# Score and value matmuls of a fused attention kernel, grouped by token tile instead of by head, with one fixed order for them on TensorE

## The chip, the cores and the metric

The kernel runs on one core of a Trainium2 chip. The metric is device time in microseconds (us), the median of the timed runs. Five engines work side by side, each through a queue of its own in order: TensorE (PE in the profile, with PEld for its weight loads), VectorE (DVE), ScalarE (ACT), GpSimd (POOL) and SyncE (SP), which issues every DMA here. They wait for each other by semaphores.

## The reference, cut to what matters

```python
B, H, S, D = q.shape                       # 2, 8, 768, 64
k_sum = k.reshape(B, H, nb, 32, D).max(axis=3)     # nb = 24 blocks
v_sum = v.reshape(B, H, nb, 32, D).mean(axis=3)
scores_l = scale * q @ k^T, masked to |i - j| < 16
scores_s = scale * q @ k_sum^T + log(32)
a = softmax over [scores_l, scores_s]
x = a @ [v, v_sum]                          # attention, (B, S, 512)
...
xk, xr = mixes of x with its left neighbour (mu_k, mu_r)
x = sigmoid(xr @ w_r) * (relu(xk @ w_k) ** 2 @ w_v)
...
u = x + (relu(x^T @ w_tok1) @ w_tok2)^T
out = u + relu(u @ w_ch1) @ w_ch2
```

The three stages follow each other. The large weights come as 64-bit floats; the kernel turns each 128x512 block into a pair of fp32r tiles (`w` high and low), and most products are three matmuls of such pairs (`mm3`).

## The kernel before, in words

**Attention.** The work is cut in 12 token tiles of 128 tokens: 6 of batch 0, then 6 of batch 1. Eight heads lie as four pairs p; in a pair, head e = 0 has its 64 values of q and k on partitions 0 to 63, head e = 1 on partitions 64 to 127. A unit is one (batch, tile, e), so there are 24 units, each with the four heads of one e.

- `s_stage`: 8 float32 matmuls into a PSUM bank `sp` (tag "s", two banks). Each has 64 rows of weights (the partitions of e) and 64 columns (half a tile of tokens), and streams 120 keys: 96 in the window and 24 block sums. The two halves of the tokens go to partitions 0 to 63 and 64 to 127 of `sp`. In the profile each float32 matmul of this kind is two records, so a unit is x16. Then per pair a DVE instruction adds the mask and takes the minimum of the negated scores (`sm`, `mn`), and ACT takes the exponential with its sum (`pe`, `den`).
- `n_stage`: DVE inverts the four sums, POOL scales the four `pe`.
- `t_stage`: four transposes on TensorE into a bank `pt`, and a copy to `PT` by DVE (batch 0) or ACT (batch 1).
- `v_stage`: 8 float32 matmuls into the bank `pv`; all 120 rows are used, the 64 columns are those of e: partitions 0 to 63 of `pv` for e = 0, 64 to 127 for e = 1. They too are two records each. After e = 1 ACT copies `pv` to `xT`.

The loop `attention` goes by units: scores of unit i, normalizing of i - 1, transposes of i - 2, values of i - 3.

**The rest on TensorE at the same time.** `main` works in chunks of 256 tokens: per chunk four groups, each of 24 matmuls `ko` (128x256, from the mixed input `xh`, `xl`), a relu and square split in `kh` and `kl`, and 12 matmuls `acc` (128x512). A chunk needs its two token tiles of attention. The first chunk also waits for the 16 weight blocks of w_k and w_v, in the order in which `Weights.step` decodes them (ACT `wst`, DVE `wf`, ACT `w` high, POOL `w` low). `gate_pass` follows with `ro`, then the token mixing (`h`, `ho`) and the channel mixing (`go`, `o`). After each of the first 8 units a filler matmul (`spin`) is put on TensorE.

**What sets the order.** The kernel is written as generators: attention yields a cost at each step and `main` is drawn on until the cost is used up. A scheduler then puts the instructions of each engine in one queue, by its own model of time and by priorities (`HS`, `HT`, `HV` and others raise one stage over another). `behind` and `after` add an order without a wait, for example of DMAs behind the last score matmul marked. Memory of the pool `at` (attention's buffers) is used again for the weights of w_r and after, so their loads wait for the last readers of those buffers.

Of the kernel before, what the change touches and what calls it, by code (L numbers as in the profile page):

```python
# [23 lines left out]
TLAG, VLAG = 2, 3  # L24
# [5 lines left out]
SPIN, SPIN_UNITS = 1, 8  # L30
# [6 lines left out]
QB = 3  # L37
# [14 lines left out]
def fused_kernel(ctx, tc, q, k, v, vt, mu, w_k, w_v, w_r, w_t1, w_t2, w_c1, w_c2, out):  # L52
# [120 lines left out]

    weights = Weights()
# [81 lines left out]
    @ahead(HL)  # L256
    def vw_load(b, t):
        ws = []
        for half in range(2):
            w = ybuf[:NC, 2 * t + half] if b == 0 else at.tile([NC, DM], F32, tag="vw", bufs=6, name="vw")  # L260
# [28 lines left out]
    @ahead(HS)  # L289
    def s_stage(u):  # L290
        b, t, e = u
        st = state[b]
        mask = masks[1 if t == 0 else 2 if t == NT - 1 else 0]
        kw, qT = st["kw"][t], st["qT"][t]
        sp = bank("s", 2, [128, NP, NC], "sp")
        mn = at.tile([128, NP], F32, tag="mn", bufs=3, name="mn")
        den = at.tile([128, NP], F32, tag="den", bufs=4, name="den")
        P = []
        r = slice(64 * e, 64 * e + 64)
        for p in range(NP):  # L300
# [6 lines left out]
        for p in range(NP):  # L307
            s = at.tile([128, NC], F32, tag="sm", bufs=4, name="sm")
            nc.vector.tensor_tensor_reduce(out=s, in0=sp[:, p], in1=mask, op0=ALU.add, op1=ALU.min,  # L309
                                           scale=-1.0 / math.sqrt(D), scalar=3.0e38, accum_out=mn[:, p:p + 1])  # L310
            pe = at.tile([128, NC], F32, tag="pe", bufs=12, name="pe")
            nc.scalar.activation(pe, s, AF.Exp, bias=mn[:, p:p + 1], scale=-1.0, accum_out=den[:, p:p + 1])  # L312
            P.append(pe)
        return {"u": u, "P": P, "den": den}

# [20 lines left out]
    def v_stage(z):  # L336
        b, t, e = z["u"]
        st = state[b]
        if e == 0:
            st["pv"][t] = bank("pv", 1, [128, NP, 128], "pv")  # L340
        pv = st["pv"][t]
        for p in range(NP):
            h = 2 * p + e
            for half in range(2):
                nc.tensor.matmul(pv[64 * e:64 * e + 64, p, 64 * half:64 * half + 64],  # L345
                                 st["vw"][t][half][0][:, h * D:(h + 1) * D],
                                 z["PT"][:, p, 64 * half:64 * half + 64], start=True, stop=True)
        if e == 1:
            c0 = b * XB + 1 + 128 * t
            nc.scalar.copy(xT[:, :, c0:c0 + 128], pv)  # L350

    units = [(b, t, e) for b in range(B) for t in range(NT) for e in range(2)]
    done_tiles = [0]
    n_units = len(units)

    def attention():
        zs = {}
        for i in range(n_units + VLAG):
            if i < n_units:
                b, t, e = units[i]  # L360
                zs[i] = s_stage(units[i])
                if i < SPIN_UNITS:
                    spin(SPIN)
                yield 0.95
                if e == 1 and t + 1 < NT:
                    kw_sums(b, t + 1)
                if t == 0 and e == 1 - b:
# [3 lines left out]
            if 0 <= i - 1 < n_units:  # L371
                n_stage(zs[i - 1])
            if 0 <= i - TLAG < n_units:
                t_stage(zs[i - TLAG])
                yield 0.43
            if 0 <= i - VLAG < n_units:
                v_stage(zs.pop(i - VLAG))
                yield 0.7
                done_tiles[0] = (i - VLAG + 1) // 2
            if i < n_units:  # L380
                if e == 0:
                    if t + 1 < NT and t + 1 not in state[b]["vw"]:
                        vw_load(b, t + 1)
                    if b and t + 2 < NT:
                        q_load(b, t + 2)
                elif t + 1 < NT:
                    vw_sums(b, t + 1)
                if b + 1 < B:
                    prep_next(b + 1, 2 * t + e)
# [431 lines left out]
```

## Time and profile before

| what | value |
|---|---|
| time, median of 3 runs | 520.48 us (520.39 to 524.9) |
| profiled execution, first to last instruction | 518.7 us |
| median of the runs less that span | 1.8 us |
| mean granted TensorE clock | 0.994 |
| PE busy | 500.0 us, 96% of the span |
| POOL, DVE busy | 205.2 and 250.7 us |

The profiled execution's own time is its span and the launch around it; the 1.8 us between its span and the median is taken for the latter. Starts and stretches below count from the span's first instruction. A matmul's record is as long as it takes from start to end, and records overlap, so what a group costs TensorE is read from start to start.

### The profile page before, as it was taken

What the parts mean: (1) busy time and instruction counts of PE and PEld (TensorE: products, weight loads), DVE (VectorE), ACT (ScalarE), POOL (GpSimd) and SP (SyncE); (2) the same over time, 40 slices, a digit from 0 to 9 for tenths busy, and PEclk for the clock granted to TensorE, in tenths of its full rate; (3) what the DMA queues carried; (4) which work ended last, traced back from release to release, by engine and by line L of the source; (5) the groups of instructions that cost most, each with busy time, mean ns of one, the idle gap of its engine ahead of it and who ended that gap; (6) DMA issues with size and microseconds to landing.
All of it is one profiled execution on the core that took longest, in us unless ns stands there. A gap on an engine that the chain in (4) does not pass through costs nothing.

```text
span 518.7 us, 7924 instructions
## 1 busy us (share of the span) xinstructions
PE 500.0 (96%) x2968; PEld 405.6 (78%) x2968; DVE 250.7 (48%) x556; ACT 204.2 (39%) x471; POOL 205.2 (40%) x298
## 2 busy tenths in 40 slices
PE   8997889999999999999999999999999999999995
PEld 3566767888789988888867788888888888888884
DVE  3869998551132667587656766443331211311112
ACT  0668669763342555446345344443211110100100
POOL 6579989972152665388523323322100000000000
PEclk9899999999999999999999999999999999999998
DMA  8999923210066000000176361000020000200002
GB/s 265 322 307 370 313 65 102 67 51 0 1 244 243 1 2 0 1 1 1 42 243 221 145 202 42 1 1 0 1 81 2 0 0 1 81 1 0 1 0 81
DMA packets 24197, 45.40 MB, mean 88 GB/s; under 512 B 2112, under 2 KB 11328, under 8 KB 24160
## 3 DMA queue, kind: packets, MB, share of 16 engines
q1 hardware_dynamic: 24160, 44.90, 26.7%
q8 instruction: 23, 0.38, 0.3%
q14 instruction: 14, 0.11, 0.1%
HBM read 41.16 MB, written 3.15 MB: 85 GB/s over the span
## 4 chain that ended last, share of the span: by engine, by line
PE 80%; POOL 7%; issue 4%; DVE 3%; DMA 2%; ACT 2%; SPq 1%; POOLq 0%; DVEq 0%; ACTq 0%
PE o L746 19%; PE go L432 19%; PE ko L432 11%; PE acc L432 10%; PE ro L432 5%; PE pv L345 3%; PE sp L303 3%; PE ho L432 3%; POOL pe L322 3%; PE h L432 2%; PE pt L328 2%; POOL w L158 2%; PE spin L511 2%; POOL tmp L421 1%; DMA xT<-in_vt_dram 1%
## 5 line engine op out<-in xcount | busy, mean ns | idle before, releaser
L432 PE MATMUL go<-u,w 128*128 128x512 f32 x432 | 106.6, 393 | 0.0
L158 POOL TENSOR_TENSOR w<-wf,w 128x512 fp32r<-128x512 f32 x50 | 65.9, 1320 | 76.9 <-ACT w L157 75.6
L432 PEld LDWEIGHTS go<-u,w 128*128 128x128 f32 x432 | 80.7, 188 | 17.6
L746 PE MATMUL o<-w,gh 128*128 128x512 f32 x288 | 89.0, 395 | 0.0
L661 DVE SCALAR_TENSOR_TENSOR gl<-go,gh 128x512 fp32r<-128x512 f32 x36 | 24.9, 691 | 121.1 <-ACT gh L660 120.9
L432 PE MATMUL ko<-xh,w 128*128 128x256 f32 x384 | 78.1, 289 | 1.6 <-ACT xh L423 0.8
L660 ACT ACTIVATE gh<-go 128x512 fp32r<-128x512 f32 x36 | 21.6, 599 | 128.7 <-PE go L432 128.7
L432 PEld LDWEIGHTS ko<-xh,w 128*128 128x128 f32 x384 | 61.8, 188 | 5.2 <-POOL w L158 1.2
L746 PEld LDWEIGHTS o<-w,gh 128*128 128x128 f32 x288 | 54.0, 188 | 12.0
L432 PE MATMUL acc<-w,kh 128*128 128x512 f32 x192 | 59.8, 401 | 0.7 <-ACT kh L446 0.6
L746 PE MATMUL o<-w,gl 128*128 128x512 f32 x144 | 55.4, 394 | 0.0
L432 PE MATMUL ko<-xl,w 128*128 128x256 f32 x192 | 54.8, 285 | 0.0
L322 POOL TENSOR_SCALAR pe<-pe,den 128x120 f32<-128x120 f32 x96 | 46.2, 499 | 6.7 <-DVE den L320 6.2
L157 ACT CAST w<-wf 128x512 fp32r<-128x512 f32 x50 | 30.9, 618 | 44.7 <-DVE wf L155 42.7
L447 POOL TENSOR_TENSOR kl<-rl,kh 128x512 fp32r<-128x512 f32 x24 | 34.6, 1443 | 34.8 <-ACT kh L446 32.6
L421 POOL TENSOR_SCALAR tmp<-xT,oms 128x256 f32<-128x256 f32 x52 | 34.0, 664 | 33.1 <-DVE xk L422 23.9
L155 DVE SCALAR_TENSOR_TENSOR wf<-wst,wf 128x512 int32<-128x512 int32 x50 | 43.3, 870 | 7.4 <-ACT wst L145 5.7
L312 ACT ACTIVATE pe<-sm,mn 128x120 f32<-128x120 f32 x96 | 37.0, 387 | 22.5 <-DVE mn L309 16.4
L445 DVE TENSOR_TENSOR rl<-rl 128x512 f32<-128x512 f32 x24 | 19.6, 818 | 46.2 <-ACT rl L444 46.2
L432 PEld LDWEIGHTS acc<-w,kh 128*128 128x128 f32 x192 | 34.3, 188 | 8.4 <-ACT kh L446 1.3
L432 PE MATMUL acc<-w,kl 128*128 128x512 f32 x96 | 36.5, 401 | 2.0 <-POOL kl L447 2.0
L422 DVE SCALAR_TENSOR_TENSOR xk<-xT,mus,tmp 128x256 f32<-128x256 f32 x52 | 35.7, 709 | 5.0 <-POOL tmp L421 5.0
(79 smaller groups left out, 722.5 us busy)
## 6 DMA issues: line engine op xcount, KB each, us to landing
wst<-in_moe_w_ch_dram SPq DMA_DIRECT2D x24, 512.0 KB
wst<-in_moe_w_k_dram SPq DMA_DIRECT2D x8, 512.0 KB
wst<-in_moe_w_v_dram SPq DMA_DIRECT2D x8, 512.0 KB
kw<-in_k_dram SPq DMA_DIRECT2D x12, 320.0 KB
wst<-in_moe_w_tok_dram SPq DMA_DIRECT2D x6, 512.0 KB
out_dram<-o SPq DMA_DIRECT2D x12, 256.0 KB
ybuf<-in_v_dram SPq DMA_DIRECT2D x12, 192.0 KB
vw<-in_v_dram SPq DMA_DIRECT2D x12, 192.0 KB
```

The lines of the kernel that those rows point to most:

```text
L155: nc.vector.scalar_tensor_tensor(wi, top, 3, wi, ALU.logical_shift_left, ALU.bitwise_or)
L157: self.rounded.append(nc.scalar.copy(hi, wf))
L158: nc.gpsimd.tensor_tensor(lo, wf, hi.bitcast(F32), ALU.subtract)
L312: nc.scalar.activation(pe, s, AF.Exp, bias=mn[:, p:p + 1], scale=-1.0, accum_out=den[:, p:p + 1])
L322: nc.gpsimd.tensor_scalar(z["P"][p], z["P"][p], den[:, p:p + 1], 1.0, ALU.mult, ALU.mult)
L421: nc.gpsimd.tensor_scalar(tmp, xT[:, d, x0 - 1:x0 - 1 + MW], om[:, d:d + 1], 1.0, ALU.mult, ALU.mult)
L422: nc.vector.scalar_tensor_tensor(xk[:, d], xT[:, d, x0:x0 + MW], mu[:, d:d + 1], tmp, ALU.mult, ALU.add)
L432: nc.tensor.matmul(o, l, r, start=(first and i == 0), stop=(last and i == 3 * n - 1))
L447: nc.gpsimd.tensor_tensor(lo, rl, hi.bitcast(F32), ALU.subtract)
L660: nc.scalar.activation(hi, o, AF.Relu)
L661: nc.vector.scalar_tensor_tensor(lo, o, 0.0, hi.bitcast(F32), ALU.max, ALU.subtract)
L746: nc.tensor.matmul(acc[t], l, r, start=(f == 0 and i == 0), stop=(f == nf - 1 and i == 2))
```

## The change

Scores: `s_stage` takes a whole tile. Its 16 matmuls fill two banks, one for each e, and the inner loop alternates e = 1 and e = 0. Values: `v_stage` takes a whole tile too, and alternates e in the same way. The minimum is written straight to `pe` and the exponential works there in place (no `sm`). Every score, transpose and value matmul goes through `in_line`, which orders it behind the one before it in the program. The loop goes by tiles: scores of tile i, then normalizing, transposes and values of tile i - 1. `QB` falls from 3 to 2, the `vw` buffers from 6 to 5, `pe` has 16 buffers instead of 12, `PT` 4 instead of 2. Two fillers stand after each of the first 4 tiles instead of one after each of the first 8 units.

```diff
+    line = []
+
+    def in_line(inst):
+
+        behind(inst, line[-1:])
+        line.append(inst)
+        return inst
...
-    def s_stage(u):
-        b, t, e = u
+    def s_stage(b, t):
...
-        sp = bank("s", 2, [128, NP, NC], "sp")
-        mn = at.tile([128, NP], F32, tag="mn", bufs=3, name="mn")
-        den = at.tile([128, NP], F32, tag="den", bufs=4, name="den")
-        P = []
-        r = slice(64 * e, 64 * e + 64)
+        sps = [bank("s", 2, [128, NP, NC], "sp") for _ in range(2)]
         for p in range(NP):
             for half in range(2):
                 c0 = half * (WC - NC)
-                m = nc.tensor.matmul(sp[64 * half:64 * half + 64, p], qT[r, p, 64 * half:64 * half + 64],
-                                 kw[r, p, c0:c0 + NC], start=True, stop=True)
+                for e in (1, 0):
+                    r = slice(64 * e, 64 * e + 64)
+                    m = in_line(nc.tensor.matmul(sps[e][64 * half:64 * half + 64, p], qT[r, p, 64 * half:64 * half + 64],
+                                                 kw[r, p, c0:c0 + NC], start=True, stop=True))
...
+                pe = at.tile([128, NC], F32, tag="pe", bufs=PEB, name="pe")
+                nc.vector.tensor_tensor_reduce(out=pe, in0=sp[:, p], in1=mask, op0=ALU.add, op1=ALU.min,
+                                               scale=-1.0 / math.sqrt(D), scalar=3.0e38, accum_out=mn[:, p:p + 1])
+                nc.scalar.activation(pe, pe, AF.Exp, bias=mn[:, p:p + 1], scale=-1.0, accum_out=den[:, p:p + 1])
...
-            nc.tensor.transpose(pt[:NC, p], z["P"][p], ident)
-        z["PT"] = at.tile([NC, NP, 128], F32, tag="PT", bufs=2, name="PT")
+            in_line(nc.tensor.transpose(pt[:NC, p], z["P"][p], ident))
+        z["PT"] = at.tile([NC, NP, 128], F32, tag="PT", bufs=PTB, name="PT")
...
+        pv = bank("pv", 1, [128, NP, 128], "pv")
         for p in range(NP):
-            h = 2 * p + e
             for half in range(2):
...
+                for e in (1, 0):
+                    h = 2 * p + e
+                    in_line(nc.tensor.matmul(pv[64 * e:64 * e + 64, p, 64 * half:64 * half + 64],
+                                             st["vw"][t][half][0][:, h * D:(h + 1) * D],
+                                             zs[e]["PT"][:, p, 64 * half:64 * half + 64], start=True, stop=True))
...
+        for i in range(len(tiles) + 1):
+            if i < len(tiles):
+                b, t = tiles[i]
+                zs[i] = s_stage(b, t)
...
+            if i:
+                for z in zs[i - 1]:
+                    n_stage(z)
+                for z in zs[i - 1]:
+                    t_stage(z)
+                    yield 0.43
+                v_stage(zs.pop(i - 1))
```

In the rows below, `sp`, `pt` and `pv` are the matmuls of scores, transposes and values, `x8` counts matmuls of one kind in a row. TensorE, batch 0, around the third and fourth tile, before:

```order
L328 MATMUL pt<-ident,pe 120x128
L303 MATMUL sp<-kw,xT 64x120 x8
L328 MATMUL pt<-ident,pe 120x128
L345 MATMUL pv<-PT,ybuf 64x64 x8
L328 MATMUL pt<-ident,pe 120x128 x2
L303 MATMUL sp<-kw,xT 64x120 x8
L328 MATMUL pt<-ident,pe 120x128 x4
L345 MATMUL pv<-PT,ybuf 64x64 x8
```

The same place now:

```order
L308 MATMUL sp<-kw,xT 64x120 x16
L338 MATMUL pt<-ident,pe 120x128 x8
L520 MATMUL spin<-ident 128x512 x2
L354 MATMUL pv<-PT,ybuf 64x64 x16
L308 MATMUL sp<-kw,xT 64x120 x16
L338 MATMUL pt<-ident,pe 120x128 x8
L354 MATMUL pv<-PT,ybuf 64x64 x16
```

Where scores, transposes and values of several units stood mixed, a tile's scores, the tile before's transposes and its values now follow each other, and the next scores stand behind those values.

TensorE, batch 1, late in attention, before (`ko` is work of `main`):

```order
L345 MATMUL pv<-PT,vw 64x64 x8
L432 MATMUL ko<-xh,w 128x256
L432 MATMUL ko<-xl,w 128x256
L432 MATMUL ko<-xh,w 128x256 x2
L432 MATMUL ko<-xl,w 128x256
L432 MATMUL ko<-xh,w 128x256
L345 MATMUL pv<-PT,vw 64x64
L432 MATMUL ko<-xh,w 128x256
L345 MATMUL pv<-PT,vw 64x64
L432 MATMUL ko<-xl,w 128x256
L345 MATMUL pv<-PT,vw 64x64
```

The scores of the eleventh tile and the transposes of the tenth, now:

```order
L441 MATMUL acc<-w,kh 128x512 x2
L441 MATMUL acc<-w,kl 128x512
L308 MATMUL sp<-kw,qT 64x120 x16
L338 MATMUL pt<-ident,pe 120x128 x8
L441 MATMUL acc<-w,kh 128x512 x2
L441 MATMUL acc<-w,kl 128x512
```

Seven values matmuls of one unit stood one by one between `ko`; now every tile's values and nearly every tile's scores stand in one piece (the tenth tile's scores are in four).

POOL (GpSimd), around the last two of the first 16 weight blocks (`w`), before:

```order
L322 TENSOR_SCALAR pe<-pe,den 128x120 x4
L158 TENSOR_TENSOR w<-wf,w 128x512
L447 TENSOR_TENSOR kl<-rl,kh 128x512
L322 TENSOR_SCALAR pe<-pe,den 128x120 x4
L158 TENSOR_TENSOR w<-wf,w 128x512
L322 TENSOR_SCALAR pe<-pe,den 128x120 x3
L158 TENSOR_TENSOR w<-wf,w 128x512
L322 TENSOR_SCALAR pe<-pe,den 128x120 x5
```

And now:

```order
L332 TENSOR_SCALAR pe<-pe,den 128x120 x4
L158 TENSOR_TENSOR w<-wf,w 128x512
L332 TENSOR_SCALAR pe<-pe,den 128x120 x4
L158 TENSOR_TENSOR w<-wf,w 128x512
L430 TENSOR_SCALAR tmp<-xT,oms 128x256 x2
L158 TENSOR_TENSOR w<-wf,w 128x512
L430 TENSOR_SCALAR tmp<-xT,oms 128x256 x2
L332 TENSOR_SCALAR pe<-pe,den 128x120 x8
```

The last `w` of the piece is the sixteenth block in both. Ahead of it on POOL stood 71 scalings `pe`, 12 `tmp` and 3 `kl`; now 56 `pe`, 10 `tmp` and 3 `kl`.

## Rows read from the trace of the kernel before

**Rows 1.** The page's part 1: busy time, share and instructions by engine.

```profile
PE 500.0 (96%) x2968; PEld 405.6 (78%) x2968; DVE 250.7 (48%) x556; ACT 204.2 (39%) x471; POOL 205.2 (40%) x298
```

**Rows 2.** Windows: stretch, length, each engine's busy time, granted clock, DMA share, GB/s.

```profile
40.00:60.00 20.00, 15.54 (x185) 13.14 (x181) 19.56 (x65) 15.64 (x52) 20.00 (x32) 1.00 1.06 362
80.00:100.00 20.00, 20.00 (x209) 16.08 (x207) 16.22 (x71) 16.68 (x60) 19.79 (x30) 1.00 0.25 75
100.00:120.00 20.00, 20.00 (x196) 17.08 (x195) 8.51 (x30) 12.02 (x33) 13.44 (x24) 1.00 0.18 52
```

**Rows 3.** Waits of TensorE, 0 to 260 us: total, times, longest.

```profile
PE pv L345 <- DVE PT L333: 3.7, 4, 1.3
```

**Rows 4.** TensorE's timeline: one unit alone (start, length, what).

```profile
43.36 1.04 PE L303 MATMUL sp<-kw,xT 64*64 64x120 f32 x16
44.33 0.65 PE L328 MATMUL pt<-ident,pe 128*120 128x128 f32 x4
...
47.92 1.15 PE L345 MATMUL pv<-PT,ybuf 120*64 120x64 f32 x16
48.99 0.43 PE L328 MATMUL pt<-ident,pe 128*120 128x128 f32 x2
```

**Rows 5.** TensorE's timeline: units of both e back to back, and a filler.

```profile
27.04 1.90 PE L345 MATMUL pv<-PT,ybuf 120*64 120x64 f32 x32
...
29.92 1.30 PE L303 MATMUL sp<-kw,xT 64*64 64x120 f32 x26
31.15 1.12 PE L511 MATMUL spin<-ident 128*128 128x512 f32 x2
```

**Rows 6.** TensorE's timeline: values matmuls one by one between `ko`.

```profile
127.70 0.33 PE L345 MATMUL pv<-PT,vw 120*64 120x64 f32 x2
127.96 0.39 PE L432 MATMUL ko<-xh,w 128*128 128x256 f32 x1
128.28 0.33 PE L345 MATMUL pv<-PT,vw 120*64 120x64 f32 x2
128.53 0.39 PE L432 MATMUL ko<-xl,w 128*128 128x256 f32 x1
```

**Rows 7.** Windows 100.85 to 156.24 us, of `ko` alone, then of `acc` alone.

```profile
100.85:156.24 55.39, 23.86 (x155) 20.25 (x155) 4.20 (x7) 1.00 0.23 80
100.85:156.24 55.39, 19.21 (x72) 12.73 (x72) 2.35 (x4) 1.00 0.23 80
```

**Rows 8.** The chain in order of time, pieces (start, length, what).

```profile
167.70 2.84 PE ko L432 x24
170.54 2.78 PE acc L432 x12
...
191.98 0.94 PE ro L432 x4
```

**Rows 9.** The page's part 5, four groups: count, busy and mean ns, idle before.

```profile
L158 POOL TENSOR_TENSOR w<-wf,w 128x512 fp32r<-128x512 f32 x50 | 65.9, 1320 | 76.9 <-ACT w L157 75.6
L322 POOL TENSOR_SCALAR pe<-pe,den 128x120 f32<-128x120 f32 x96 | 46.2, 499 | 6.7 <-DVE den L320 6.2
L421 POOL TENSOR_SCALAR tmp<-xT,oms 128x256 f32<-128x256 f32 x52 | 34.0, 664 | 33.1 <-DVE xk L422 23.9
L312 ACT ACTIVATE pe<-sm,mn 128x120 f32<-128x120 f32 x96 | 37.0, 387 | 22.5 <-DVE mn L309 16.4
```

**Rows 10.** POOL's timeline, with idle time before and what ended it.

```profile
36.62 1.39 POOL L322 TENSOR_SCALAR pe<-pe,den 128x120 f32<-128x120 f32 x4 [1.37 <-DVE den L320]
39.98 0.94 POOL L421 TENSOR_SCALAR tmp<-xT,oms 128x256 f32<-128x256 f32 x2 [1.98 <-ACT xT L350]
...
99.47 1.27 POOL L158 TENSOR_TENSOR w<-wf,w 128x512 fp32r<-128x512 f32 x1
```

**Rows 11.** SP's timeline: the loads of w_r. ACT's: the fourth block of w_r.

```profile
143.33 1.77 SPq L130 DMA_DIRECT2D wst<-in_moe_w_r_dram  x4
...
184.43 0.62 ACT L157 CAST w<-wf 128x512 fp32r<-128x512 f32 x1 [1.82 <-DVE wf L155]
```

**Rows 12.** Tile `pt`: DVE's copy to `PT`, ns min/median/max, first and last start.

```profile
L333 DVE COPY PT<-pt x12: 677/682/692, 25.0 to 75.6; 120x512 f32<-120x512 f32 x12
```

More of the change, by code (lines that the diff above doesn't have):

```diff
@@ L259, in vw_load @@
         for half in range(2):
-            w = ybuf[:NC, 2 * t + half] if b == 0 else at.tile([NC, DM], F32, tag="vw", bufs=6, name="vw")
+            w = ybuf[:NC, 2 * t + half] if b == 0 else at.tile([NC, DM], F32, tag="vw", bufs=VB, name="vw")
             row, srow = (NB, 0) if half == 0 else (0, NK)
@@ L302, in s_stage @@
                 c0 = half * (WC - NC)
-                m = nc.tensor.matmul(sp[64 * half:64 * half + 64, p], qT[r, p, 64 * half:64 * half + 64],
-                                 kw[r, p, c0:c0 + NC], start=True, stop=True)
+                for e in (1, 0):
+                    r = slice(64 * e, 64 * e + 64)
+                    m = in_line(nc.tensor.matmul(sps[e][64 * half:64 * half + 64, p], qT[r, p, 64 * half:64 * half + 64],
+                                                 kw[r, p, c0:c0 + NC], start=True, stop=True))
         if PINL:
             mark.append(m)
[L307 to L314, printed above, removed]
+        zs = []
+        for e, sp in enumerate(sps):
+            mn = at.tile([128, NP], F32, tag="mn", bufs=4, name="mn")
+            den = at.tile([128, NP], F32, tag="den", bufs=4, name="den")
+            P = []
+            for p in range(NP):
+                pe = at.tile([128, NC], F32, tag="pe", bufs=PEB, name="pe")
+                nc.vector.tensor_tensor_reduce(out=pe, in0=sp[:, p], in1=mask, op0=ALU.add, op1=ALU.min,
+                                               scale=-1.0 / math.sqrt(D), scalar=3.0e38, accum_out=mn[:, p:p + 1])
+                nc.scalar.activation(pe, pe, AF.Exp, bias=mn[:, p:p + 1], scale=-1.0, accum_out=den[:, p:p + 1])
+                P.append(pe)
+            zs.append({"u": (b, t, e), "P": P, "den": den})
+        return zs
     @ahead(HN)
@@ L335, in v_stage @@
     @ahead(HV)
-    def v_stage(z):
-        b, t, e = z["u"]
+    def v_stage(zs):
+        b, t, _ = zs[0]["u"]
         st = state[b]
-        if e == 0:
-            st["pv"][t] = bank("pv", 1, [128, NP, 128], "pv")
-        pv = st["pv"][t]
+        pv = bank("pv", 1, [128, NP, 128], "pv")
         for p in range(NP):
-            h = 2 * p + e
             for half in range(2):
[L345 to L352, printed above, removed]
+                for e in (1, 0):
[3 more added lines that the diff above has]
+                                             zs[e]["PT"][:, p, 64 * half:64 * half + 64], start=True, stop=True))
+        c0 = b * XB + 1 + 128 * t
+        nc.scalar.copy(xT[:, :, c0:c0 + 128], pv)
+    tiles = [(b, t) for b in range(B) for t in range(NT)]
     done_tiles = [0]
-    n_units = len(units)
     def attention():
         zs = {}
[L358 to L362, printed above, removed]
+        for i in range(len(tiles) + 1):
+            if i < len(tiles):
+                b, t = tiles[i]
+                zs[i] = s_stage(b, t)
+                if i < SPIN_TILES:
                     spin(SPIN)
                 yield 0.95
-                if e == 1 and t + 1 < NT:
+                if t + 1 < NT:
                     kw_sums(b, t + 1)
-                if t == 0 and e == 1 - b:
+                if t == 0:
                     if b == 0:
@@ L370, in attention @@
                     vw_sums(b, 0)
[L371 to L377, printed above, removed]
-                yield 0.7
[L379 to L382, printed above, removed]
+                yield 0.95
+            if i:
[5 more added lines that the diff above has]
+                v_stage(zs.pop(i - 1))
+                yield 0.7
+                done_tiles[0] = i
+                yield 0.7
+            if i < len(tiles):
+                if t + 1 < NT:
+                    if t + 1 not in state[b]["vw"]:
                         vw_load(b, t + 1)
-                    if b and t + 2 < NT:
-                        q_load(b, t + 2)
-                elif t + 1 < NT:
                     vw_sums(b, t + 1)
+                if b and t + 2 < NT:
+                    q_load(b, t + 2)
                 if b + 1 < B:
-                    prep_next(b + 1, 2 * t + e)
+                    for e in range(2):
+                        prep_next(b + 1, 2 * t + e)
     def prep_next(b, j):
```

8 lines of the change are left out of this document (4 added, 4 removed).

## The prediction

> **What bounds the kernel now.** I read the busy shares first: TensorE is busy 500.0 of 518.7 us [rows 1], so work taken from it can shorten the run, but only in a stretch where nothing else sets the pace. The windows of 20 us show where that is. From 40 to 60 us POOL is busy for all 20.00 us and DVE for 19.56, while TensorE has 15.54; from 80 to 100 TensorE (20.00) and POOL (19.79) are both full; from 100 to 120 POOL falls to 13.44 and TensorE stays full [rows 2]. So TensorE alone sets the pace only from about 100 us on. What ends the earlier stretch is on POOL's timeline: the sixteenth weight block starts at 99.47 us and ends at 100.74 [rows 10]. Before it, `main` can't leave its first chunk, so TensorE has little to do but attention.
>
> **What the scores and values cost, and what alternation can give.** A unit of scores alone takes 0.97 us from its start to the next group's (43.36 to 44.33), a unit of values 1.07 (47.92 to 48.99) [rows 4]. Scores of e = 0 and e = 1 ran into each other at one place: 26 records took 1.30 us where 16 alone take 1.04 [rows 4, 5]. Ten more records cost 0.26 us, 26 ns each, against (1.04 - 0.26) / 15 = 52 ns alone (the last record's 0.26 us taken off, an estimate of its length). That is a factor of two, with the heads' rows of the array working side by side. For values 32 records took 1.90 us, where two units apart take 2.14 [rows 4, 5]: an overlap at the seam alone. I take the full factor for both: a tile's 16 score matmuls in the time of one unit, 1.06 us (0.97 and a little for entering and leaving), its values in 1.07. Bounds for a tile: scores 1.0 to 1.94, values 1.07 to 2.14. If all of it counted, 12 x (0.88 + 1.07) = 23 us would go.
>
> **Pieces.** Where values stand one by one between `ko`, a pair recurs every 0.58 us (127.70, 128.28) [rows 6]. A `ko` costs 2.84 / 24 = 0.118 [rows 8], so one values matmul costs 0.46 instead of 1.07 / 8 = 0.13: going in and out costs 0.32 us. In the stretch after 100.85 us (below) attention's records at their price in a row, 56 x 0.052 + 28 x 0.11 + 128 x 0.067 = 14.6 us, fill 20.4 us, so entering and leaving is some 6 us there. [...]
>
> **The part that counts, step by step.** I compare the moment when TensorE gets past the sixteenth block and is full from then on, and the attention work left at it.
>
> First, the moment. Before, it is 100.85 us, where `ko` goes on just after the block [rows 7]. POOL's order now has 15 scalings and 2 `tmp` fewer ahead of the sixteenth block: 15 x 0.499 + 2 x 0.664 = 8.8 us [rows 9]. With the idle that POOL has now, the block would end at 100.74 - 8.8 = 91.9. The new line costs some of this. Values now stand right behind their transposes, so TensorE waits for the copy to `PT` (0.68 us [rows 12]; such waits take up to 1.3 us today, four in 3.7 us [rows 3]), and the next tile's scores, so DVE, ACT and then POOL, wait behind that. POOL lost 1.37 us for `den` and 1.98 for `xT` in the same stretch [rows 10]. I take 1 us for each of tiles 2 to 5 before POOL's backlog covers it: 4 us, between 0 and 10. So 95.9 for the block. The eighth tile's transposes, which TensorE meets then, need 2 `tmp` and 3 scalings more: 2 x 0.664 + 3 x 0.499 = 2.8, so 98.7. TensorE isn't late there: ahead of this point its queue has 9 tiles of scores (9.5 us), 59 transposes at 0.11 (0.65 us for 4, 0.43 for 2 [rows 4]; 6.5), 7 of values (8.9 with 0.2 for the piece), 16 filler records of about 0.53 (8.5) [rows 5], 96 `ko` (11.4) and 36 `acc` at 2.78 / 12 = 0.232 (8.3) [rows 8]: 53 us from 11.8, so it could be there at 65. The 9 x 0.88 + 7 x 1.07 = 15 us saved on TensorE before this point go into longer waits. First term: 98.7 - 100.85 = -2.2 us.
>
> Second, what is left. Before, the stretch from 100.85 to attention's last values at 156.24 takes 55.39 us and holds 155 `ko` and 72 `acc` [rows 7]; less 155 x 0.118 and 72 x 0.232 that leaves 20.4 us for attention: 56 records of scores, 28 transposes, 128 records of values, and their pieces. Now, from the eighth tile's transposes on: 3 tiles of scores at 1.06, one of them in four pieces (3 x 0.32 more), 4.1; 37 transposes at 0.11, 4.1; 5 tiles of values at 1.07 and 0.2, 6.4: together 14.6. TensorE has then done 96 `ko` instead of 86 and the same 36 `acc`, another 10 x 0.118 = 1.2. Second term: 14.6 - 1.2 - 20.4 = -7.0 us.
>
> The stages after attention hold the same instructions and stand in the same order but for a few `ro` and `ko`, and TensorE's queue is nearly without gaps there: nothing. `sm` gone, more `pe` and `PT` buffers, one `qT` fewer: DVE and ACT do the same instructions, and the loads of `qT` and `vw` are behind scores that now come two tiles ahead of use, so their landing stays hidden; if it doesn't, the slower case below has it. The fillers are as many as before and lie where TensorE isn't the bound.
>
> Sum: -2.2 - 7.0 = -9.2 us against the profiled execution: a span of 509.5. With 1.8 us around it, as the median of the runs stands to the span now, **511.3 us**.
>
> **Rivals.**
>
> *POOL's shorter list counts in full (faster still).* No new waits: the block ends at 91.9, first term -6.2, time 507.3; with scores cheaper than the 1.06, and TensorE rather than POOL late in the early stretch, down to 504. For it: 12 buffers of `pe` become 16 and TensorE has slack. Against: DVE is at 19.56 of 20 us from 40 to 60 [rows 2], so a wait there isn't made up.
>
> *Alternation doesn't overlap.* The only overlap in the trace was between whole units. If matmuls that alternate one by one stay at 52 ns a record, scores keep 1.94 and values 2.14 a tile: the second term rises by 3 x 0.88 + 5 x 1.07 = 8.0, to +1.0, time 519.3, no change. Against it stand the 26 ns [rows 5]. [...]
>
> *w_r comes late.* Its loads are issued at 143.33, behind the last scores, and its fourth block is rounded at 184.43 [rows 11], 41.1 us later; the first `ro` is at 191.98 [rows 8], 48.7 us after the issue. In the new order 123 `ko`, 60 `acc` and the end of attention (4.7 us) lie between: 14.5 + 13.9 + 4.7 = 33.1 us. If the 41 us were needed, TensorE would wait 8 us: 519.3. Against: the decoding stands behind the same steps of `main` on ACT in both orders, so its lateness looks like order and not like the loads.
>
> *The one line makes attention a chain (slower).* Scores of a tile wait for the values of two tiles before. Once round: scores 1.06, eight exponentials 8 x 0.387, the last four scalings 2.0, transposes 0.44, copy 0.68, values 1.07, some 0.7 for `den` and semaphores: 9.0 us for two tiles, 4.5 for one. POOL itself needs 8 x 0.499 + 2 x 1.32 = 6.6 us a tile [rows 9], so the chain has 2.1 us of room. It decides once queueing on DVE, ACT and POOL puts more than that on each tile; at 3.1 us more than POOL's own, on each of batch 0's six tiles, 18.6 us replace the 4 above: 511.3 + 14.6 = 525.9. For it: DVE's 19.56 of 20 us. Against: two tiles are in flight and the `main` work in between is small.
>
> **How the numbers follow.** My forecast has 0.50, POOL's full gain 0.18, no overlap 0.12, w_r 0.10, the chain 0.10. A measurement of this kernel tells about 1% (5.2 us) from no change. Faster by more than that: 0.45 of the forecast's 0.50 (the other 0.05 has 8 to 10 us of waits in place of 4: 515.3 to 517.3) and 0.18: 0.63. Within 1%: 0.05, 0.12, 0.09 of w_r and 0.02 of the chain: 0.28. Slower: 0.08 of the chain and 0.01 of w_r: 0.09. The range goes from 504 (the low end of the first rival) to 519.5 (waits at their bound, no overlap and w_r); beyond lie the chain and some of the rest, less than 2 in 10.
>
> **What would show it.** In the new trace: a tile's 32 score records in about 1.1 us and its 32 values records in about 1.1 to 1.3 (if near 2, no overlap); POOL's sixteenth `w` ending at 92 to 99; TensorE without waits over 0.3 us after that until 250; more waiting before 95 us than now, `pv` for `PT` and `ko` for `w`; the end of attention's values with 312 `ko` done; the first `ro` without a wait for `w`. I am wrong if POOL is idle over 10 us between 30 and 95, or if score and value groups take the time of two units.

## The result and the profile after

The changed kernel takes 526.77 us (median of 8 runs, 525.84 to 527.98), against 521.25 for the kernel before in the same job: a ratio of 1.0098, 95% interval 1.0072 to 1.0124. It is slower by 1%, outside the range and on the other side of the forecast. The profiled execution has a span of 525.2 us, where before had 518.7.

TensorE's busy time fell as it should. The page's busy line of the changed kernel, to be set beside [rows 1]:

```profile
PE 486.2 (93%) x2968; PEld 394.2 (75%) x2968; DVE 248.6 (47%) x556; ACT 202.7 (39%) x471; POOL 203.9 (39%) x298
```

TensorE does 13.8 us less work and the run is 6.5 us longer, so some 20 us of waiting are new. The windows of 20 us show where, in the columns of [rows 2]:

```profile
40.00:60.00 20.00, 8.17 (x112) 5.73 (x107) 11.45 (x38) 10.56 (x29) 10.94 (x16) 0.62 0.95 338
...
80.00:100.00 20.00, 17.88 (x149) 14.51 (x148) 15.34 (x45) 11.38 (x33) 16.66 (x28) 0.91 0.18 46
100.00:120.00 20.00, 15.93 (x194) 13.36 (x193) 12.37 (x54) 13.82 (x46) 16.81 (x29) 0.91 0.19 54
120.00:140.00 20.00, 20.00 (x166) 16.81 (x165) 4.43 (x8) 5.92 (x11) 7.77 (x11) 1.00 0.08 25
```

From 40 to 60 us no engine is busy for more than 11.45 of 20 us; the DMA engines alone are full, with a share of 0.95 (1.06 before). Before, POOL had 20.00 there and DVE 19.56 [rows 2]. A stretch in which all engines idle has a chain of waits through all of it. TensorE's granted clock is 0.62 there, after 1.00 before. Whether the idling or the low clock comes first, the windows don't say.

The overlap is there. TensorE's timeline of the changed kernel, one tile's scores and one tile's values:

```profile
155.00 1.05 PE L308 MATMUL sp<-kw,qT 64*64 64x120 f32 x32
155.98 1.09 PE L338 MATMUL pt<-ident,pe 128*120 128x128 f32 x8
...
161.97 1.15 PE L354 MATMUL pv<-PT,vw 120*64 120x64 f32 x32
163.05 0.73 PE L441 MATMUL acc<-w,kh 128*128 128x512 f32 x2
```

Both heads' 32 score records take 0.98 us to the next group's start (155.00 to 155.98), and both heads' values 1.08: the time that one head took [rows 4]. So the price of a tile was right. The time at which the early stretch ends was not. POOL's timeline around the sixteenth weight block, which answers to [rows 10], and TensorE's at the eighth tile's transposes:

```profile
105.36 1.27 POOL L158 TENSOR_TENSOR w<-wf,w 128x512 fp32r<-128x512 f32 x1
106.60 0.94 POOL L430 TENSOR_SCALAR tmp<-xT,oms 128x256 f32<-128x256 f32 x2
107.50 1.45 POOL L158 TENSOR_TENSOR w<-wf,w 128x512 fp32r<-128x512 f32 x1
```

```profile
112.00 0.32 PE L338 MATMUL pt<-ident,pe 128*120 128x128 f32 x1 [1.80 <-POOL pe L332]
113.40 0.81 PE L338 MATMUL pt<-ident,pe 128*120 128x128 f32 x2 [1.08 <-POOL pe L332]
```

The block ends at 108.95 (95.9 forecast), and TensorE is past its last wait at 113.40 (98.7 forecast), 4.45 us after the block instead of 2.8. From there to attention's last values at 181.15 the windows of `ko` alone and of `acc` alone answer to [rows 7]:

```profile
113.40:181.15 67.75, 30.35 (x217) 28.30 (x217) 5.36 (x9) 0.98 0.25 78
113.40:181.15 67.75, 27.35 (x108) 19.48 (x108) 3.51 (x6) 0.98 0.25 78
```

67.75 - 217 x 0.118 - 108 x 0.232 leaves 17.1 us for attention. The first term is thus 113.40 - 100.85 = +12.55 us instead of -2.2; the second 17.1 - 1.2 - 20.4 = -4.5 instead of -7.0. Their sum, +8.05, is 1.5 us more than the spans' difference; the 1.5 us lie behind attention, and their cause stays open.

**Where the early time went.** The chain of waits of the changed kernel passes through DMA in this stretch, where that of before ran through `pe` and `w` on POOL. Pieces in order of time (start, length, what):

```profile
44.58 9.96 DMA kw<-in_k_dram
54.54 0.02 issue
54.57 0.69 DVE ks L231
55.25 0.34 DVE wf L149
55.59 0.07 DVE ks L231
55.66 0.49 issue
56.15 0.47 DVE xk L431
56.62 0.08 DVE den L329
```

And the rows on DVE's and POOL's timelines that this chain joins:

```profile
54.57 0.69 DVE L231 TENSOR_REDUCE ks<-kw 128x16 f32<-128x512 f32 x1 [4.90 <-DMA kw<-in_k_dram]
...
58.36 4.22 POOL L332 TENSOR_SCALAR pe<-pe,den 128x120 f32<-128x120 f32 x8 [7.28 <-DVE den L330]
```

Here `ks` holds the block maxima of the second batch's keys (`k_max`, line 231). POOL first uses them at 85.09 us. But in DVE's queue two such rows now stand ahead of the fourth tile's denominators and of the rest of `xk`, the first chunk's input. Their keys land at 54.54, 9.96 us after the issue, so DVE idles 4.90 us, POOL 7.28 us for `den`, and TensorE for `xh`. Before, the first `ks` stood behind that chunk's `xl` and came at 55.01 without waiting:

```profile
53.51 1.58 DVE L424 TENSOR_TENSOR xl<-xk,xh 128x1024 fp32r<-128x1024 f32 x1
55.01 0.67 DVE L223 TENSOR_REDUCE ks<-kw 128x16 f32<-128x512 f32 x1
```

No line of the diff touches `k_max`. The scheduler moved it, because the other work moved.

Another long wait stands just before. TensorE waits 6.02 us for the third tile's values. The view names ACT's `w`, but what ends last is DVE's second copy to `PT`, at 49.67, behind a `wf` and the next tile's masks:

```profile
48.99 0.68 DVE L343 COPY PT<-pt 120x512 f32<-120x512 f32 x1
...
49.77 1.98 PE L354 MATMUL pv<-PT,ybuf 120*64 120x64 f32 x32 [6.02 <-ACT w L157]
```

### The profile page after: what moved, and what is told of

It is laid out like the page before. It is cut to its first block, busy times and chain, and to the rows that moved or that the text cites. A ratio compares the mean times of both kernels' runs of the same rounds, so it can differ in the third digit from the quotient of the medians.

```text
span 525.2 us, 7839 instructions
## 1 busy us (share of the span) xinstructions
PE 486.2 (93%) x2968; PEld 394.2 (75%) x2968; DVE 248.6 (47%) x556; ACT 202.7 (39%) x471; POOL 203.9 (39%) x298
## 4 chain that ended last, share of the span: by engine, by line
PE 75%; DMA 9%; DVE 6%; POOL 4%; issue 2%; ACT 2%; SPq 2%; POOLq 0%; DVEq 0%; ACTq 0%
PE o L755 19%; PE go L441 19%; PE ko L441 11%; PE acc L441 11%; PE ro L441 6%; DMA ybuf<-in_v_dram 3%; PE ho L441 3%; PE h L441 2%; POOL pe L332 2%; DMA kw<-in_k_dram 2%; DMA wst<-in_moe_w_v_dram 2%; DMA wst<-in_moe_w_k_dram 2%; DVE wf L149 1%; POOL w L158 1%; DVE xk L431 1%
## 5 line engine op out<-in xcount | busy, mean ns | idle before, releaser
L441 PE MATMUL ko<-xh,w 128*128 128x256 f32 x384 | 79.8, 295 | 5.6 <-ACT xh L432 4.7
L441 PEld LDWEIGHTS ko<-xh,w 128*128 128x128 f32 x384 | 64.2, 195 | 7.9 <-ACT xh L432 5.0
L441 PE MATMUL ko<-xl,w 128*128 128x256 f32 x192 | 55.6, 290 | 0.0
L332 POOL TENSOR_SCALAR pe<-pe,den 128x120 f32<-128x120 f32 x96 | 43.2, 470 | 23.9 <-DVE den L330 19.5
L321 ACT ACTIVATE pe<-pe,mn 128x120 f32<-128x120 f32 x96 | 36.7, 385 | 33.3 <-DVE mn L319 33.1
L456 POOL TENSOR_TENSOR kl<-rl,kh 128x512 fp32r<-128x512 f32 x24 | 33.2, 1382 | 31.7 <-ACT kh L455 30.4
L155 DVE SCALAR_TENSOR_TENSOR wf<-wst,wf 128x512 int32<-128x512 int32 x50 | 39.4, 796 | 11.0 <-ACT wst L145 9.2
L431 DVE SCALAR_TENSOR_TENSOR xk<-xT,mus,tmp 128x256 f32<-128x256 f32 x52 | 34.0, 686 | 10.9 <-POOL tmp L430 10.7
L441 PEld LDWEIGHTS ko<-xl,w 128*128 128x128 f32 x192 | 37.6, 196 | 0.9
```

Of the source, the lines that this page charges most:

```text
L155: nc.vector.scalar_tensor_tensor(wi, top, 3, wi, ALU.logical_shift_left, ALU.bitwise_or)
L321: nc.scalar.activation(pe, pe, AF.Exp, bias=mn[:, p:p + 1], scale=-1.0, accum_out=den[:, p:p + 1])
L332: nc.gpsimd.tensor_scalar(z["P"][p], z["P"][p], den[:, p:p + 1], 1.0, ALU.mult, ALU.mult)
L431: nc.vector.scalar_tensor_tensor(xk[:, d], xT[:, d, x0:x0 + MW], mu[:, d:d + 1], tmp, ALU.mult, ALU.add)
L441: nc.tensor.matmul(o, l, r, start=(first and i == 0), stop=(last and i == 3 * n - 1))
L456: nc.gpsimd.tensor_tensor(lo, rl, hi.bitcast(F32), ALU.subtract)
```

## The experiments

Three theories stood after the two traces. A: single places in DVE's queue, `ks` first of all. B: TensorE's granted clock fell and made the chain long. C: the tile as a unit, or the strict line, is the wrong grain. The kernel before was run beside every one of them; ratios are to it.

**First round: the source changed, the scheduler free.**

`e1_maxima_late`: the second batch's `ks` behind a later mark.

```
-        nc.vector.tensor_reduce(st["ks"][:, :, n * t:n * t + n], keys, AX.X, ALU.max)
+        m = nc.vector.tensor_reduce(st["ks"][:, :, n * t:n * t + n], keys, AX.X, ALU.max)
+        if b:
+            after(m)
...
-        if j >= 6 and j % 2 == 0:
-            k_max(b, j // 2 - 3)
...
-            for t in (3, 4, 5):
+            for t in range(NT):
                 k_max(b, t)
```

> The changed kernel with one thing moved: all six block maxima (ks) of the second batch are queued behind the sixth tile's scores instead of the fourth tile's, so that on VectorE nothing that waits for a keys load (5.5 us there) stands ahead of the fourth tile's denominators and the first chunk's xk. Theory A (this wait in VectorE's queue is what lost the early time): VectorE's idle 4.9 us and GpSimd's 7.3 us go, the 16th w ends near 101 to 104 instead of 109.0, span 518 to 521 (525.2 now). Theory B (TensorE's granted clock, 0.62 from 40 to 60 us, makes the chain long by itself): w ends within 2 us of 109, the clock stays at 0.6 to 0.7, span 523 to 526. Theory C (the tile is the wrong grain: its scores need both banks, so each tile runs masks, exp, scaling, transposes and values one after the other): the idle time turns up in front of other instructions, span 522 to 526, and the clock stays low since TensorE still idles some 20 us before 113.

Measured: 525.59 us, ratio 1.0073 (1.0046 to 1.0100), span 523.5; the sixteenth `w` at 103.5. The block comes when theory A expected it; the span, the clock (0.66 from 40 to 60 us) and the idle time that turns up elsewhere are what theory C expected. The fourth tile's denominators no longer wait for the keys, but TensorE's waits moved to other names: 6.0 us before one `pv`, and 5.2 us before a filler that now stands behind the first `ko` group and needs its bank:

```profile
PE pv L356 <- ACT w L157: 6.0, 1, 6.0
PE spin L520 <- ACT rl L453: 5.2, 1, 5.2
```

Moving one thing in the source moved the rest of the order too, so this run decides neither on A nor on C.

`e2_fillers`:

```
-SPIN, SPIN_TILES = 2, 4
+SPIN, SPIN_TILES = 4, 6
```

> The changed kernel with 4 fillers behind each of six tiles' scores instead of 2 behind each of four: 24 instead of 8, some 18 us more work for TensorE at full clock, against the 24.8 us that it idles between 20 and 113 us. Theory B (clock): granted clock 40 to 80 back to 0.9 to 1.0, 16th w at 100 to 104, span 517 to 521. Theories A and C (waits in the queues, the clock only follows): the clock rises but the idle time only fills, w still ends at 107 to 112, span 524 to 530.

Measured: 515.33 us, ratio 0.9877 (0.9847 to 0.9906), span 512.4, the sixteenth `w` at 95.1. This looks like theory B, and better than it asked for. The granted clock rose to 0.91, 0.74, 1.00 and 1.00 in the windows from 20 to 100 us (0.80, 0.62, 0.69 and 0.91 in the changed kernel).

`e4_no_alternation`: the loop over the two heads outermost, in `s_stage` as shown and in `v_stage` likewise.

```
-        for p in range(NP):
-            for half in range(2):
-                c0 = half * (WC - NC)
-                for e in (1, 0):
+        for e in (1, 0):
+            for p in range(NP):
+                for half in range(2):
+                    c0 = half * (WC - NC)
```

> The changed kernel with the matmuls of a tile in the order of before within the tile (head 1's 8 pairs, then head 0's) and all else as changed: the tile as a unit and the strict line stay, the alternation goes. If overlap of the two quadrants is the gain of the change: 32 scores in 1.6 to 2.0 us instead of 1.05, 32 values in 1.9 instead of 1.15; from 113 us on three tiles' scores and five tiles' values are left, so 3 x 0.6 to 0.9 + 5 x 0.75, 5 to 6 us more, and 1 to 3 us in the early chain: span 530 to 534. If the queues hide it: within 1.5 us of 525.2.

Measured: 531.94 us, ratio 1.0189 (1.0136 to 1.0242): 5.2 us above the changed kernel, as the overlap theory has it. The scheduler was free, but its order stayed nearly that of the changed kernel: on ACT the same, on DVE and TensorE but for a few instructions.

`h1_first_batch_units`: `attention` runs the first batch with the stages of before and the second with those of after.

```
+        for i in range(2 * NT):
+            t, e = divmod(i, 2)
+            zs[i] = su_stage((0, t, e))
...
+        for t in range(NT + 1):
+            if t < NT:
+                cur = s_stage(1, t)
```

> The first batch by single heads with transposes and values two and three steps later, as before the change; the second batch by tiles, alternating, in one line, as after it. If the loss lies in the early stretch alone and the alternation pays in the second batch: 16th w at 100 to 102, the attention behind it 4.4 to 7 us shorter than before, span 511 to 515, ratio to before 0.985 to 0.993. If the tile as a unit costs waits wherever it stands (theory C): TensorE waits over 0.3 us in the second batch of 4 us or more, ratio 0.997 to 1.005.

Measured: 517.03 us, ratio 0.9924 (0.9897 to 0.9952), the sixteenth `w` at 99.0. TensorE's waits from 96 to 200 us add up to 0.3 us, so the tile as a unit costs nothing in the second batch: against theory C. The ratio and the span (515.0) are at the edge of what was expected.

**Second round: is it the clock or the order?** The fillers of `e2_fillers` had also changed most of DVE's, ACT's and TensorE's order. To part the two, the order of one kernel was written out as a table and imposed on another, each instruction behind its predecessor on its engine, so that the scheduler has nothing left to choose.

```
+        for a_, b_ in zip(row, row[1:]):
+            tc.add_manual_dep(b_, a_.name,
+                              mybir.DependencyInfo(mybir.DependencyClass.NoSync, mybir.DependencyReason.DATA), reason="queue order")
```

`f2_fillers_out_same_order`: the table of `e2_fillers`, `SPIN, SPIN_TILES = 2, 4`.

> All five engines' queues in exactly the order of the run with 24 fillers (515.33 us, span 512.4), written out as a table, and of its 24 fillers only the first two behind each of the first four tiles' scores left, as in the changed kernel. Clock theory: granted clock falls to 0.6 to 0.8 between 20 and 80 us, 16th w at 102 to 109 instead of 95.1, 522 to 527 us. Order theory (the fillers only moved the scheduler to a better order of the other instructions): 513 to 517 us, w within 2 us of 95.

Measured: 516.55 us, ratio 0.9909 (0.9880 to 0.9938), the sixteenth `w` at 96.9. The clock fell to 0.76, 0.59, 0.84 and 0.91 in the windows from 20 to 100 us, about as low as in the changed kernel, and the time rose by only 1.2 us. This run decides against theory B.

`f1_fillers_in_same_order`: the table of the changed kernel, with

```
-SPIN, SPIN_TILES = 2, 4
+SPIN, SPIN_TILES = 6, 4
```

> All five engines' queues in exactly the order of the changed kernel (526.77 us, span 525.2), written out as a table, with 6 fillers instead of 2 at each of its four places, 16 more in all (19 us at full clock, 0.59 us a record). Clock theory: clock at 0.9 to 1.0 between 20 and 60 us, 16th w at 100 to 104 instead of 109.0, 516 to 521 us. Order theory: w at 107 to 112, 525 to 531 us.

Measured: 527.87 us, ratio 1.0128 (1.0091 to 1.0164), the sixteenth `w` at 108.6. Two windows of this run, then two rows of DVE and POOL, show why:

```profile
20.00:40.00 20.00, 18.37 (x181) 10.73 (x175) 15.75 (x60) 15.20 (x54) 14.93 (x32) 1.00 1.07 310
40.00:60.00 20.00, 6.66 (x71) 4.73 (x70) 11.97 (x45) 9.22 (x28) 9.14 (x13) 0.61 0.88 319
```

```profile
53.06 0.69 DVE L255 TENSOR_REDUCE ks<-kw 128x16 f32<-128x512 f32 x1 [6.69 <-DMA kw<-in_k_dram]
...
56.85 3.18 POOL L356 TENSOR_SCALAR pe<-pe,den 128x120 f32<-128x120 f32 x5 [9.08 <-DVE den L354]
```

The clock stands at 1.00 up to 40 us (0.80 in the changed kernel) and the first three tiles' values come some 3 us earlier (46.47 instead of 49.77 for the third). Then DVE waits 6.69 us for the keys instead of 4.90, POOL 9.08 instead of 7.28, and half of the lead is gone (56.85 against 58.36); at the sixteenth `w` nearly all of it is (108.6 against 108.95). From 40 to 60 us the clock was 0.61 with the fillers too, so this run tests it only up to 40 us. Nor did imposing a table as such make the kernel faster here. With both runs theory B has fallen as the main cause: the fillers helped because the scheduler came out with another order.

`e1e2_both`: `ks` late as in `e1_maxima_late`, and 24 fillers, the scheduler free.

> The second batch's block maxima late (as in the first run) together with 24 fillers. If the wait for the keys load costs something once the clock is held: 1 to 4 us below the run with 24 fillers alone, 511 to 514.5 us. If the clock was all: 514 to 517 us.

Measured: 517.75 us, ratio 0.9932 (0.9908 to 0.9955), above both expectations. It is another order again, and tells nothing of `ks` alone.

`b24_before_fillers`: in the kernel before,

```
-SPIN, SPIN_UNITS = 1, 8
+SPIN, SPIN_UNITS = 2, 12
```

> The kernel before with 24 fillers instead of 8 (two behind each of its first 12 units). Its granted clock is 0.94 to 1.00 already. Clock theory: nothing to win, 521 to 526 us, the same or some us slower. If fillers help by themselves in this kernel, whatever the change: 515 to 518 us.

Measured: 534.02 us, ratio 1.0248 (1.0217 to 1.0279). With them TensorE is busy for 59.16 of the 60 us from 20 to 80. Fillers don't help by themselves. The run is 12.9 us slower with some 19 us more of them, but the scheduler was free here too, so the fillers' part in this isn't told apart from that of another order.

**Third round: single places in a fixed order.**

`f3_only_maxima_moved`: the changed kernel's table, three rows of DVE's queue moved.

```
-L231 TENSOR_REDUCE ks<-kw
 L149 TENSOR_SCALAR wf<-wst
-L231 TENSOR_REDUCE ks<-kw
 L431 SCALAR_TENSOR_TENSOR xk<-xT,mus,tmp
 L329 TENSOR_SCALAR den<-den
...
 L433 TENSOR_TENSOR xl<-xk,xh
-L231 TENSOR_REDUCE ks<-kw
...
 L343 COPY PT<-pt
+L231 TENSOR_REDUCE ks<-kw x3
```

> All queues in exactly the order of the changed kernel (526.77 us, span 525.2) but for three rows of VectorE: the second batch's first three block maxima (ks), which stand ahead of the first chunk's xk and the fourth tile's denominators there, stand behind the fifth tile's masks and one PT copy, as in the order that gave 515.33 and 516.55 us. Theory A2 (this place in VectorE's queue is what the lost time hangs on): the 4.9 us of VectorE's idle time and the 7.3 us of GpSimd's go, the fifth tile's last score matmul and the first ko come at 52 to 54 instead of 58.2, 16th w at 101 to 104 instead of 109.0, 518 to 522 us. Rival (the rest of the order is as bad): 524 to 527 us, w at 106 to 110.

Measured: 521.93 us, ratio 0.9983 (0.9947 to 1.0018), span 520.4, the sixteenth `w` at 103.9. Three rows are worth 4.8 us in the span and in the median (6.0 by the two ratios), and the interval doesn't touch the changed kernel's. Theory A holds for this place. In the profiled executions 1.5 of the block's 5.0 us stood ahead of the edit already (POOL's first `w` begins at 33.41 instead of 34.93); the 4.8 us of the medians are from 10 and 8 runs.

What is next on the chain is again in DVE's queue, in this run's chain of waits:

```profile
55.82 1.26 POOL w L182
57.08 0.02 issue
57.10 1.49 DVE wf L173
58.59 0.19 DVE pe L343
58.78 0.01 DVE mn L343
58.79 0.60 DVE PT L367
59.39 1.78 DVE ks L255 x3
61.17 1.66 DVE vrs L277
62.83 0.34 DVE wf L173
```

A first half of `wf` (line 173 of that kernel) waits for POOL's `w`, since there are two buffers; behind it stand the copies of the fourth tile's transposes, the three `ks` and the sums `vrs`. TensorE's values and POOL's next `w` wait for what is behind:

```profile
64.61 1.74 PE L378 MATMUL pv<-PT,ybuf 120*64 120x64 f32 x32 [4.90 <-ACT w L181]
...
64.55 1.69 POOL L182 TENSOR_TENSOR w<-wf,w 128x512 fp32r<-128x512 f32 x1 [6.25 <-ACT w L181]
```

The first row names ACT's `w`; the last thing the values need is the second copy to `PT`, at 63.83 on DVE. Here the name that the view gives is not the cause.

`f4_maxima_moved_fillers`: the same with `SPIN, SPIN_TILES = 6, 4`.

> As the run before it (three maxima moved, all else in the order of the changed kernel), with 6 fillers instead of 2 at each of the four places. In the changed order the fillers brought the tiles ahead of 50 us forward by 2 to 4 us, and the wait for the keys load took it back (fourth tile's scaling began at 56.9 against 58.4). Theory A2 with the clock behind it: without that wait the 2 to 4 us stay, 515 to 519 us, 16th w at 98 to 101. If the clock is worth nothing even so: the same as the run before it within 1 us, or slower by the fillers' work.

Measured: 523.81 us, ratio 1.0029 (0.9998 to 1.0059). With the wait for the keys gone, fillers and clock together still give nothing. The clock was 1.00 instead of 0.83 from 20 to 40 us, and 0.74 as before from 40 to 60 (mean of the profiled execution 0.978 instead of 0.972). POOL's `w` of 64.55 came at 63.13, but the sixteenth at 104.3 instead of 103.9.

`f6_same_order_no_alternation`: the table of `e2_fillers`, its 24 fillers, and the heads' loop outermost as in `e4_no_alternation`, head 0 first.

> All queues in exactly the order of the run with 24 fillers (515.33 us, 16th w at 95.1), but within each tile head 0's matmuls first and then head 1's. Overlap theory: 32 scores in 1.6 to 1.9 us instead of 1.05 and 32 values in 1.9 instead of 1.15; five tiles' scores and seven tiles' values lie behind the 16th w there: 5 x 0.6 to 0.85 + 7 x 0.75 = 8.3 to 9.5 us, and 0 to 3 us ahead of it: 523 to 528 us. If the alternation is hidden by the queues: 515 to 517 us.

Measured: 522.43 us, ratio 1.0005 (0.9973 to 1.0037), 7.1 us above `e2_fillers`, just below what the overlap theory gave. TensorE's timeline of this run:

```profile
162.35 1.51 PE L331 MATMUL sp<-kw,qT 64*64 64x120 f32 x32
...
169.03 1.90 PE L377 MATMUL pv<-PT,vw 120*64 120x64 f32 x32
```

Scores that only stand head behind head take 1.51 us a tile, less than the two units' 1.94: 1.51 - 1.05 = 0.46 us of overlap to be had by alternating, not 0.6 to 0.85. Values take 1.90 against 1.15, as said. 5.4 tiles of scores and 7 of values behind the block: 5.4 x 0.46 + 7 x 0.75 = 7.7 us. In the profiled execution (525.25 us) the block itself ended at 98.4 instead of 95.1.

`e3_no_line`: without the two lines of `in_line` that make the row.

```
-        behind(inst, line[-1:])
-        line.append(inst)
```

> The changed kernel without the strict line: alternation and tiles stay, and the scheduler is free to mix scores, transposes and values. If the strict line costs (the next tile's scores wait for the values of the tile before): 519 to 523 us. If the loss hangs on single places of the order: 522 to 530 us, wherever the maxima come to stand; a later place of the maxima than the fourth tile's denominators goes with under 522.

Measured: 519.48 us, ratio 0.9949 (0.9909 to 0.9989). In this order the first late `ks` runs at 55.6, behind the fifth tile's scores. It waits 3.57 us for the keys there too, and the run is 7.3 us faster than the changed kernel all the same. Without the line the whole order is another, so what the line costs in itself isn't shown; the orders of `e2_fillers` and `f2_fillers_out_same_order` keep it and are faster.

**Fourth round: the rest of the first term.**

`f5_maxima_and_copies`: as `f3_only_maxima_moved`, and in DVE's queue

```
+L343 COPY PT<-pt x2
 L149 TENSOR_SCALAR wf<-wst
 L319 pe,mn<-sp,mask
-L343 COPY PT<-pt
-L231 TENSOR_REDUCE ks<-kw x3
-L253 TENSOR_REDUCE vrs<-ybuf
...
-L343 COPY PT<-pt
 L155 SCALAR_TENSOR_TENSOR wf<-wst,wf
 L330 RECIPROCAL den<-den x2
+L231 TENSOR_REDUCE ks<-kw x3
+L253 TENSOR_REDUCE vrs<-ybuf
```

> The order of the changed kernel with the three maxima moved (521.93 us, 16th w at 103.9), and in VectorE's queue one more place turned round: the fourth tile's two PT copies go ahead of the wf that waits 2.4 us for GpSimd's w, and the three maxima and the sums vrs (3.6 us) behind both halves of that wf. In the run before, the fourth tile's values began at 64.6, 7.3 us behind its last transpose (57.3), since the second copy came at 63.8; GpSimd idled 6.25 us at 58.3 for a w whose second wf half came at 63.1. If these places in VectorE's queue are the rest of the loss: values at 58.5 to 60, GpSimd's idle 6.25 down to 2 or 3, 16th w at 99 to 101, 516.5 to 519.5 us. Rival (the next wait takes it up, the masks or transposes of the fifth tile are late anyway): 520.5 to 523 us.

Measured: 516.19 us, ratio 0.9887 (0.9849 to 0.9925), the sixteenth `w` at 100.4. The rows of TensorE and POOL that answer to the two above:

```profile
60.47 1.15 PE L378 MATMUL pv<-PT,ybuf 120*64 120x64 f32 x32
...
61.26 1.28 POOL L182 TENSOR_TENSOR w<-wf,w 128x512 fp32r<-128x512 f32 x1 [2.21 <-ACT w L181]
```

These rows are from an execution of 519.74 us. The values come 4.1 us earlier, POOL idles 2.21 instead of 6.25, and the median falls by 5.7 us (5.0 by the two ratios).

`f9_copies_of_two_tiles`: also

```
+L343 COPY PT<-pt x2
 L149 TENSOR_SCALAR wf<-wst
 L319 pe,mn<-sp,mask x6
...
-L343 COPY PT<-pt
...
-L343 COPY PT<-pt
```

> As the run before it, and the fifth tile's two PT copies also ahead of the next wf that waits 2.9 us for GpSimd's w and of the sixth tile's masks: there the values began at 77.4, 5.9 us behind the last transpose. If each such place costs: another 2 to 4 us, 513.5 to 517 us. If GpSimd (w and scaling in one row) is the bound by then: within 1 us of the run before it.

Measured: 517.85 us, ratio 0.9928 (0.9894 to 0.9961): no gain, the rival. In the profiled execution the fifth tile's values came 2.8 us earlier and POOL's sixteenth `w` at 98.4; but its first `w` had already ended 1.5 us earlier (33.9 against 35.4), so 1.3 and 0.5 us are left for the edit. POOL's row there is filled by the copies of `ks` into `kw`:

```profile
74.42 6.30 POOL L260 TENSOR_SCALAR kw<-ks 128x96 f32<-128x96 f32 x12 [1.29 <-DVE ks L254]
80.70 0.71 POOL L355 TENSOR_SCALAR pe<-pe,den 128x120 f32<-128x120 f32 x2
```

`f8_best_order_copies`: the table of `e2_fillers`, with the same two pairs of copies moved ahead.

> The order that came out with 24 fillers (515.33 us, 16th w at 95.1), with the fourth and the fifth tile's PT copies moved ahead in VectorE's queue: of the fourth's, the second ahead of three maxima and a wf pair (values at 56 instead of 59.9), of the fifth's, both ahead of the sixth tile's masks (80 instead of 82.9). If early values are worth their time there: 511 to 514 us. If GpSimd's row of w, scaling and kw copies sets the 16th w at 95 by then: 514.5 to 516.5 us.

Measured: 514.97 us, ratio 0.9880 (0.9847 to 0.9914), the sixteenth `w` at 94.1: within the noise of `e2_fillers`. These two beat the kernel before by 1.2%.

## Why the prediction was wrong

The second term and the price behind it were right in kind. A tile's scores take 1.05 us (1.06 said) and its values 1.15 (1.07). Alternation alone gives 7.1 us in a fixed order. The term measured -4.5 us for -7.0: the mean clock of 0.98 over the stretch would make 67.75 x 0.02 = 1.4 of the missing 2.5 us, and the other 1.1 isn't told apart.

The removed work was right too. POOL's busy time up to the end of the sixteenth block, in the kernel before and in the changed one (the last of the five pairs of numbers):

```profile
0.00:100.74 100.74, 90.07 (x814) 64.61 (x814) 79.42 (x280) 65.35 (x216) 84.37 (x173) 0.98 0.76 229
0.00:108.95 108.95, 80.05 (x706) 55.06 (x708) 72.69 (x236) 55.89 (x179) 73.49 (x156) 0.81 0.66 200
```

POOL has 84.37 - 73.49 = 10.9 us less work (8.8 forecast). But its idle time there rose from 16.37 to 35.46 us, by 19.1, where the forecast had put 4. That the block ends at 94.1 to 96.9 in the best orders, near the 95.9 forecast, is no confirmation: POOL has 43 scalings ahead of it in `e2_fillers` and 56 in the changed kernel.

The step that failed is the first term's new waits: "1 us for each of tiles 2 to 5 [...] 4 us, between 0 and 10". By the same reckoning they came to 4 + 13.1 = 17 us (the block at 108.95 instead of 95.9), beyond the bound; 1.6 us more came between the block and the eighth tile's transposes. The price was taken from waits of the kernel before, the four for `PT` [rows 3] and two of POOL [rows 10]. These price a wait by what is awaited: a copy of 0.68 us. What they can't price is what the waiting row holds up behind it, nor what stands ahead of the copy in DVE's queue: TensorE's wait for the third tile's values alone is 6.02 us. Two places in DVE's queue made most of it: the `ks` that wait for a load (4.8 us in the median, `f3_only_maxima_moved`) and the copies, `ks` and `vrs` queued behind a `wf` that waits for POOL (5.7 us, `f5_maxima_and_copies`). Together they are 10.6 of the 11.8 us between the changed kernel and the best run; the last 1.2 us weren't resolved. Against the forecast more is open. With both places repaired the block ended at 100.4, 4.5 us behind the forecast, and the third tile's values still waited 6.0 us; no run moved that copy.

The prediction had said that DVE and ACT do "the same instructions". It does, in another order, and that was passed over: `ks` stood ahead of `xk` and `den` in the order of the new program before any run.

The slower rival came closest in time, 525.9, and it named queueing on DVE. Its mechanism was another: 3.1 us on each of six tiles, through a line that binds the scores to values two tiles back. The waits stood at a few places of batch 0, and with two of them repaired the strict line runs at 516.2. So its queueing was right, and that its time came near is luck. No overlap has fallen (`f6_same_order_no_alternation`). 32 score records in 0.98 us are 31 ns each, where that rival kept 52. A late `w_r` has fallen too: TensorE has no wait from 114 to 250 us in the changed kernel. POOL's full gain didn't come.

Of the signs listed, the records' times and the absence of later waits came as said. "I am wrong if POOL is idle over 10 us between 30 and 95" is what the trace showed: 65 - 44.03 = 21.0 us (5.1 before), 9.06 of it from 40 to 60 and 7.28 at one row.

```profile
30.00:95.00 65.00, 45.32 (x458) 34.85 (x459) 46.72 (x153) 40.00 (x121) 44.03 (x71) 0.75 0.60 193
```

## What to carry to other kernels

When a change lets a scheduler order the work anew, read the new queues for rows that wait for a load or for another engine, and price each by all that stands behind it, not by the awaited thing. When a knob helps, hold the order fixed and turn the knob alone before crediting the knob: the fillers gained 11.4 us, and with the order held they were worth 1.2 at most. A chain of waits that passes through a DMA whose data nobody needs yet points at a row to move.

## What the runs showed of the hardware

In the changed kernel TensorE's granted clock was 0.62 from 40 to 60 us, where TensorE was busy for 8.17 of 20 us, and 0.69 in the next 20 us, where a tile's values took 1.97 us (at 69.58) against 1.15 at 161.97, in a stretch at 1.00. That was not what the time hung on. With the clock at 1.00 instead of 0.80 from 20 to 40 us the changed order took 527.87 us (`f1_fillers_in_same_order`), and with 0.59 from 40 to 60 the order of `e2_fillers` still took 516.55 (`f2_fillers_out_same_order`).

Scores of the two heads overlap in part without alternation (32 records in 1.51 us in `f6_same_order_no_alternation`, where alternating takes 1.05 in the changed kernel and two units apart 1.94 in the kernel before); values hardly do (1.90, 1.15 and 2.14 in the same three). The traces don't say why the two differ.
